# Six shared PSUM banks, attention three chunks ahead and an earlier first layer, in attention followed by a squared-ReLU layer pair

## The chip, the cores and the metric

The kernel runs on one core of a Trainium2 chip. The metric is the time of one execution on the device in microseconds (us). Each kernel was executed several times beside executions of the kernel before on the same chip. The engines are named as in the profile: PE is the matmul engine, DVE the vector engine, ACT the scalar engine, POOL the one that issues the loads, SP the one that issues the stores. PSUM is the memory that the matmuls write to; the kernels here divide it into eight banks, and a pool of PSUM tiles with `bufs=n` holds n tiles in turn. A tile is reused once its last reader is done with it. "Span" is the time from the first to the last instruction of a profiled execution; it was about 2 us less than the time of that execution.

## The reference

Attention over 4 batches of 8 heads, 768 positions, head size 64, with a mask that keeps the first 8 positions and the last 96, and a bias that falls with distance; then two layers on the 3072 tokens of 512 features:

```python
keep = is_global | is_local                      # 8 global keys, 96 local ones
a = softmax(where(keep, q @ k.T / 8 - slope[h] * dist, -1e9))
x = (a @ v).transpose(0, 2, 1, 3).reshape(3072, 512)
h = np.maximum(x @ w_in, 0.0)                    # 512 -> 2048
out = h * h @ w_out                              # 2048 -> 512
```

The kernel computes it in 12 chunks of 256 positions, three to a batch (u = 0, 1, 2). The first chunk of a batch (u = 0) needs no keys or values of other chunks; the other two need a second key tile (`kb`) and a second value tile (`veven`).

## The kernel before

Per chunk, a job list of attention is woven into a job list of the two layers. The schedule is fixed by hand, so the order of jobs is the order of their matmuls on PE: in the timeline below `trk` waits 0.68 us, and the `hps` put down after it starts only then. `later` holds vector work that is put down just before the next job.

```python
ps_sc  = tile_pool("ps_sc",  bufs=2)   # scores: 2 tiles of two banks
ps_ffn = tile_pool("ps_ffn", bufs=3)   # both layers (and the turns of chunks 0 and 1)
ps_att = tile_pool("ps_att", bufs=1)   # ALL other attention tiles: one bank

def turn_q(c): trq = ps_att.tile(...)  # 8 transposes -> ACT copy to qx; later: 2 DVE copies
def turn_k(c): trk = ps_att.tile(...)  # 8 transposes -> ACT copy to kx; later: 4 DVE copies (kb)
def fix_v(c):  ...                     # DVE: vodd and, for u != 0, veven
def score(c, a):
    sp = ps_sc.tile([P, 2, 2, 2, P])   # 8 matmuls
    nc.scalar.activation(out=ex, in_=sp, func=AF.Exp)       # 128x1024
    later.append(phat = ex * mask)                          # DVE
def attend(c, a):
    av = ps_att.tile(...)              # 8 matmuls of phat with V
    rec = 1 / av[..., D]; tm = av * rec                     # DVE
def to_x(c, g):
    trx = ps_att.tile(...)             # 4 matmuls of tm with a permutation -> ACT copy to xt
def first(c, i):                       # 8 matmuls -> ACT relu (hr), later: DVE square (h2)
    ps = ps_ffn.tile(...)
def second(c, j, m0):                  # 4 matmuls of 512 columns; after 16, DVE copy y and store
    if m0 == 0: ck.yps = ps_ffn.tile(...)
# ... cut ...
run(<attention of chunk 0, then of chunk 1>)                # the ramp
run(merge(zip_jobs(f1(0), f1(1)) + f2(0) + f2(1), prep(2) + [fix_v(2)] + att[2], 20, 30))
run(merge(f1(2), prep(3) + [fix_v(3)] + att[3] + prep(4) + [fix_v(4)], 0, 7))
for c in range(2, NC):
    main = zip_jobs(f2(c), f1(c + 1)) if c + 1 < NC else f2(c)
    side = att[c + 2] ...              # with prep(c + 3) and fix_v(c + 3) in between
    run(merge(main, side, 1, len(main) - 2))                # side spread evenly over main
```

The softmax here doesn't subtract the row's maximum and nothing guards it: scores larger than these inputs give would overflow.

Of the kernel before, what the change touches and what calls it, by code (L numbers as in the profile page):

```python
# [8 lines left out]
FP32 = mybir.dt.float32  # L9
# [5 lines left out]
P = 128  # L15
# [3 lines left out]
def merge(main, side, start, stop):  # L19

    out = []
    done = 0
    for i, f in enumerate(main):
        if i >= start:
            want = len(side) if i >= stop else (i - start) * len(side) // (stop - start)
            while done < want:
                out.append(side[done])
                done += 1
        out.append(f)
    return out + side[done:]  # L30
# [3 lines left out]
def kernel(  # L34
# [32 lines left out]
    stage_p = ctx.enter_context(tc.tile_pool(name="stage", bufs=4))  # L67
    sv_p = ctx.enter_context(tc.tile_pool(name="svp", bufs=7))
# [6 lines left out]
    ps_sc = ctx.enter_context(tc.tile_pool(name="ps_sc", bufs=2, space=bass.MemoryType.PSUM))  # L75
    ps_ffn = ctx.enter_context(tc.tile_pool(name="ps_ffn", bufs=3, space=bass.MemoryType.PSUM))
    ps_att = ctx.enter_context(tc.tile_pool(name="ps_att", bufs=1, space=bass.MemoryType.PSUM))
# [9 lines left out]
    dist = const.tile([P, 2, 3, P], FP32, name="dist")  # L87
    loc = const.tile([P, 2, 3, P], FP32, name="loc")
# [15 lines left out]
    def fill_index():  # L104
        nc.gpsimd.iota(pidx, pattern=[[0, 1]], base=0, channel_multiplier=1,
                       allow_small_or_imprecise_dtypes=True)
        for kind, base in ((0, 0), (1, P)):
            for ek in range(2):
                nc.gpsimd.iota(dist[:, ek, kind, :].rearrange("p (e c) -> p e c", e=2),
                               pattern=[[1, 2], [2, HP]], base=base - ek,  # L110
                               channel_multiplier=-2, allow_small_or_imprecise_dtypes=True)
        nc.gpsimd.iota(jmp, pattern=[[1, P]], base=0, channel_multiplier=-2,
                       allow_small_or_imprecise_dtypes=True)

    def fill_masks():
# [14 lines left out]
        V.tensor_scalar(out=dist[:, :, 2, :], in0=dist[:, :, 0, :], scalar1=shift,  # L130
                        scalar2=None, op0=ALU.add)
        for k0, k1, f in ((0, 2, 0), (2, 3, 1)):
            d, l, g = dist[:, :, k0:k1, :], loc[:, :, k0:k1, :], ge0[:, :, k0:k1, :]
            V.tensor_scalar(out=g, in0=d, scalar1=0.0, scalar2=None, op0=ALU.is_ge)
            V.scalar_tensor_tensor(out=l, in0=d, scalar=float(NL), in1=g,
                                   op0=ALU.is_lt, op1=ALU.mult)
            V.scalar_tensor_tensor(out=d, in0=d, scalar=fill[:, f:f + 1], in1=l,
                                   op0=ALU.subtract, op1=ALU.mult)
            V.tensor_scalar(out=d, in0=d, scalar1=fill[:, f:f + 1], scalar2=None,
                            op0=ALU.add)  # L140
        V.tensor_scalar(out=perm, in0=jmp, scalar1=thr, scalar2=None, op0=ALU.is_equal)

# [26 lines left out]
    def load(c, h0=0, h1=H):  # L169
        ck = chunks[c]  # L170
        if h0 == 0:
            ck.sq = stage_p.tile([P, H, P], FP16, name="sq", tag="sq")
            ck.sk = stage_p.tile([P, H, P], FP16, name="sk", tag="sk")
            ck.sv = sv_p.tile([P, H, P], FP16, name="sv", tag="sv")
        for src, dst in ((q, ck.sq), (k, ck.sk), (v, ck.sv)):
            nc.gpsimd.dma_start(  # L176
                out=dst[:, h0:h1, :],
                in_=src[ck.b, h0:h1, ck.u * CH:(ck.u + 1) * CH, :].rearrange(
                    "h (p e) d -> p h (e d)", e=2))

    def turn_q(c, h0=0, h1=H, ramp=False):
        ck = chunks[c]
        if h0 == 0:
# [3 lines left out]
        trp = (ps_ffn.tile([P, H, P], FP16, name="trq", tag="ffn") if ramp  # L187
               else ps_att.tile([P, H, P], FP16, name="trq", tag="att"))
# [261 lines left out]
```

## Time and profile before

| | before |
|---|---|
| three runs | 296.85, 297.13, 301.64 us |
| span of the profiled run, mean granted clock | 300.0 us, 0.965 |
| first matmul of the first layer | 39.6 us |
| a chunk of the steady part, u = 0 / u = 1, 2 | 20.2 / 23.8 us |
| PE work in such a chunk, without waits (summed in the prediction) | 17.8 us |

A run is called slow when it is over 1.5% above the fastest of its kernel; the profiled one (302.07 us) was.

The page of the profiled run. The first line is busy time, share of the span and number of instructions of each engine; the rows below are tenths of busy time, and of the granted matmul clock, in 40 equal slices of the span.

```profile
PE 237.9 (79%) x2208; PEld 157.7 (53%) x2208; DVE 154.5 (51%) x407; ACT 144.4 (48%) x211; POOL 41.0 (14%) x58
...
PE   1353489968757896998897896998897996999995
...
PEclk9999999999997999899998899899999899799999
```

PE is busy for 79%, but its row shows a thin ramp in the first five slices, and the clock row dips to 7 and 8 now and then. The windows view says how much time each stretch has. Its columns are the stretch and its length, then busy time (with the number of instructions) of PE, of PE's weight loads, of DVE, ACT and POOL, then the granted clock, the DMA share and GB/s.

```profile
core 0: us, PE busy (x) PEld busy (x) DVE busy (x) ACT busy (x) POOL busy (x), PEclk, DMA share, GB/s
0.00:39.63 39.63, 15.12 (x177) 11.73 (x178) 21.52 (x64) 21.05 (x34) 22.11 (x37) 1.00 1.25 166
125.40:145.64 20.24, 18.30 (x186) 12.18 (x185) 10.72 (x26) 11.23 (x17) 2.62 (x3) 1.00 0.49 66
145.64:169.47 23.83, 20.00 (x186) 12.85 (x185) 12.91 (x35) 11.34 (x17) 2.62 (x3) 0.93 0.41 56
```

In the first 39.6 us PE works 15. Then a chunk with u = 0 takes 20.2 us and one with u = 1 or 2 takes 23.8, the latter at a clock of 0.93. The timeline of PE inside the last of these shows why (start, length, instructions; in brackets the idle time just ahead of the group and what ended it):

```profile
155.02 0.41 PE L285 MATMUL av<-vodd,phat 128*128 128x65 f16 x8
155.27 1.02 PE L346 MATMUL yps<-w_out_sb,h_1527 128*128 128x512 f16 x4
156.97 0.61 PE L206 MATMUL trk<-ident,sk 128*128 128x128 f16 x8 [0.68 <-DVE tm L292]
157.41 1.04 PE L334 MATMUL hps<-xt,w_in_sb 128*128 128x256 f16 x8
...
162.44 0.40 PE L304 MATMUL trx<-perm,tm 128*128 128x128 f16 x4 [2.00 <-DVE tm L292]
162.68 1.49 PE L346 MATMUL yps<-w_out_sb,h_1527 128*128 128x512 f16 x4
163.95 1.92 PE L334 MATMUL hps<-xt,w_in_sb 128*128 128x256 f16 x8
165.66 1.46 PE L346 MATMUL yps<-w_out_sb,h_1814 128*128 128x512 f16 x4
```

The transposes of k (`trk`) wait 0.68 us for `tm` of an attend that was done a block earlier: they have no use for `tm`, but they share its bank. Then PE idles 2.0 us before the last `trx`, which does need `tm`. And the blocks after it run slow: 1.49 us in place of 1.02 to 1.04, then 1.92, then 1.46. Waits of this kind in the whole run (total us, times, longest):

```profile
PE trx L304 <- DVE tm L292: 13.6, 8, 2.2
...
PE av L285 <- DVE tm L292: 8.9, 13, 1.4
...
PE trk L206 <- DVE tm L292: 4.7, 7, 0.7
```

### The profile page before, as it was taken

What the parts mean: (1) busy time and instruction counts of PE and PEld (TensorE: products, weight loads), DVE (VectorE), ACT (ScalarE), POOL (GpSimd) and SP (SyncE); (2) the same over time, 40 slices, a digit from 0 to 9 for tenths busy, and PEclk for the clock granted to TensorE, in tenths of its full rate; (3) what the DMA queues carried; (4) which work ended last, traced back from release to release, by engine and by line L of the source; (5) the groups of instructions that cost most, each with busy time, mean ns of one, the idle gap of its engine ahead of it and who ended that gap; (6) DMA issues with size and microseconds to landing.
All of it is one profiled execution on the core that took longest, in us unless ns stands there. A gap on an engine that the chain in (4) does not pass through costs nothing.

```text
span 300.0 us, 5337 instructions
## 1 busy us (share of the span) xinstructions
PE 237.9 (79%) x2208; PEld 157.7 (53%) x2208; DVE 154.5 (51%) x407; ACT 144.4 (48%) x211; POOL 41.0 (14%) x58
## 2 busy tenths in 40 slices
PE   1353489968757896998897896998897996999995
PEld 0243368634545564565564464566565564666662
DVE  4565525365363865374466366274466366274321
ACT  0867436353564563464463463464463463363320
POOL 8833350030301212012012000000000000000000
PEclk9999999999997999899998899899999899799999
DMA  7999999193380947019147010000010000000001
GB/s 70 145 206 207 198 181 179 10 120 86 69 79 2 106 50 93 35 8 126 45 70 72 35 38 2 35 0 37 36 37 0 37 35 2 35 37 35 37 35 70
DMA packets 45191, 20.26 MB, mean 68 GB/s; under 512 B 38000, under 2 KB 42096, under 8 KB 45168
## 3 DMA queue, kind: packets, MB, share of 16 engines
q0 software_dynamic: 41712, 13.63, 41.1%
q1 hardware_dynamic: 3456, 6.29, 5.5%
q8 instruction: 17, 0.28, 0.4%
q14 instruction: 6, 0.05, 0.0%
HBM read 27.26 MB, written 6.29 MB: 112 GB/s over the span
## 4 chain that ended last, share of the span: by engine, by line
PE 55%; DVE 21%; ACT 16%; issue 6%; POOL 1%; ACTq 0%; POOLq 0%
PE hps L334 22%; PE yps L346 20%; ACT ex L268 7%; DVE tm L292 5%; DVE phat L271 4%; PE av L285 3%; PE sp L262 3%; ACT hr L337 3%; ACT kx L208 2%; PE trx L304 2%; PE trk L206 2%; PE trq L190 2%; ACT qx L192 1%; DVE rec L290 1%; ACT mask L145 1%
## 5 line engine op out<-in xcount | busy, mean ns | idle before, releaser
L334 PE MATMUL hps<-xt,w_in_sb 128*128 128x256 f16 x768 | 104.4, 286 | 0.0
L337 ACT ACTIVATE hr<-hps 128x512 f16<-128x512 f32 x96 | 57.8, 602 | 85.1 <-PE hps L334 85.1
L334 PEld LDWEIGHTS <-w_in_sb 128*128 128x128 f16 x768 | 75.9, 102 | 18.9 <-issue 2.9
L268 ACT ACTIVATE ex<-sp 128x1024 f16<-128x1024 f32 x48 | 46.5, 1022 | 13.1 <-PE sp L262 13.1
L271 DVE TENSOR_TENSOR phat<-ex,mask 128x1024 f16<-128x1024 f16 x48 | 33.1, 692 | 26.1 <-ACT ex L268 26.0
L285 PE MATMUL av<-vodd,phat 128*128 128x65 f16 x256 | 19.7, 205 | 26.2 <-DVE phat L271 10.5
L285 PEld LDWEIGHTS <-phat 128*128 128x128 f16 x384 | 17.7, 103 | 38.4 <-DVE phat L271 16.5
L350 DVE COPY y<-yps 128x512 f32<-128x512 f32 x24 | 16.5, 689 | 17.5 <-PE yps L346 17.3
L176 POOL DMA_DIRECT2D sq<-in_q_dram x13 | 11.3, 870 | 89.3 <-PE trq L190 83.3
L306 ACT CAST xt<-trx 128x512 f16<-128x512 f32 x24 | 14.1, 587 | 18.2 <-PE trx L304 17.6
L304 PE MATMUL trx<-perm,tm 128*128 128x128 f16 x96 | 10.5, 239 | 13.9 <-DVE tm L292 13.6
L292 DVE TENSOR_TENSOR tm<-av,rec 128x256 f16<-128x256 f32 x48 | 20.4, 424 | 1.7
L262 PE MATMUL sp<-qx,kx 64*128 64x128 f16 x256 | 15.8, 234 | 6.4 <-ACT kx L208 5.8
L208 ACT COPY kx<-trk 128x1024 f16<-128x1024 f16 (+1 forms) x13 | 12.3, 949 | 14.2 <-PE trk L206 14.2
L262 PEld LDWEIGHTS <-kx 64*128 64x128 f16 x256 | 10.5, 102 | 13.7 <-issue 6.7
L304 PEld LDWEIGHTS <-tm 128*128 128x128 f16 x96 | 6.9, 105 | 18.9 <-DVE tm L292 16.6
L192 ACT COPY qx<-trq 128x1024 f16<-128x1024 f16 (+1 forms) x13 | 12.4, 955 | 6.9 <-PE trq L190 6.9
L176 POOL DMA_DIRECT2D sk<-in_k_dram x13 | 11.2, 860 | 21.7 <-PE trk L206 16.1
L290 DVE RECIPROCAL rec<-av 128x4 f32<-128x4 f32 x48 | 8.6, 180 | 9.9 <-PE av L285 9.7
L206 PE MATMUL trk<-ident,sk 128*128 128x128 f16 x96 | 8.4, 234 | 6.5 <-DVE tm L292 4.7
L190 PE MATMUL trq<-ident,sq 128*128 128x128 f16 x96 | 8.4, 234 | 5.5 <-DMA sq<-in_q_dram 4.7
L206 PEld LDWEIGHTS <-sk 128*128 128x128 f16 x96 | 6.5, 105 | 10.8 <-issue 10.2
(82 smaller groups left out, 288.0 us busy)
## 6 DMA issues: line engine op xcount, KB each, us to landing
out_dram<-y SPq DMA_DIRECT2D x24, 256.0 KB, 2.0
sq<-in_q_dram POOLq DMA_DIRECT2D x11, 256.0 KB, 4.7
sk<-in_k_dram POOLq DMA_DIRECT2D x11, 256.0 KB, 6.3
sv<-in_v_dram POOLq DMA_DIRECT2D x11, 256.0 KB, 6.9
w_in_sb<-in_moe_w_in_dram POOLq DMA_DIRECT2D x4, 512.0 KB, 12.7
w_out_sb<-in_moe_w_out_dram POOLq DMA_DIRECT2D x4, 512.0 KB, 18.4
sq<-in_q_dram POOLq DMA_DIRECT2D x2, 128.0 KB, 3.4
sk<-in_k_dram POOLq DMA_DIRECT2D x2, 128.0 KB, 3.5
```

The lines of the kernel that those rows point to most:

```text
L176: nc.gpsimd.dma_start(out=dst[:, h0:h1, :], in_=src[ck.b, h0:h1, ck.u * CH:(ck.u + 1) * CH, :].rearrange("h (p e) d -> p h (e d)", e=2))
L206: nc.tensor.transpose(out=trp[:, h, :], in_=ck.sk[:, h, :], identity=ident)
L208: nc.scalar.copy(out=ck.k[:, hh, :], in_=trp[:, hh, :])
L262: nc.tensor.matmul(sp[:, ek, e, s, :], lhsT=ck.keys[rr][rows, h, :], rhs=ck.q[rows, 1 - ek:3 - ek, h, rr * HP:(rr + 1) * HP], start=True, ...
L268: nc.scalar.activation(out=ex.rearrange("p k e c -> p (k e c)"), in_=sp.rearrange("p k e s c -> p (k e s c)"), func=AF.Exp, scale=scale)
L271: later.append(lambda: nc.vector.tensor_tensor(out=phat, in0=ex, in1=mask[:, :, 2 * a:2 * a + 2, k0:k0 + 2, :].rearrange("p k e s c -> p k ...
L285: nc.tensor.matmul(av[:, e, rr, :], lhsT=phat[:, ek, e, s * P:(s + 1) * P], rhs=ck.vals[rr][:, 2 * a + e, ek, 0:D + 1], start=ek == 0, sto ...
L292: nc.vector.tensor_tensor(out=tm.rearrange("p r e d -> p e r d"), in0=av[:, :, :, 0:D], in1=rec[:, :, :, None].to_broadcast([P, 2, 2, D]), ...
L304: nc.tensor.matmul(trx[:, i, rr, :], lhsT=ck.tm[2 * g + i][:, rr, :, :], rhs=perm, start=True, stop=True)
L334: nc.tensor.matmul(ps[:, m2, :], lhsT=w_in_sb[:, kk, m * P:(m + 1) * P], rhs=ck.xt[:, kk, :], start=kk == 0, stop=kk == NCT - 1)
L337: nc.scalar.activation(out=hr, in_=ps, func=AF.Relu)
L346: nc.tensor.matmul(ck.yps, lhsT=ck.h2[:, m, j * P:(j + 1) * P], rhs=w_out_sb[:, m, :], start=m == 0, stop=m == NFT - 1)
```

## The change

The intent: let attention tiles and first-layer tiles rotate through six single banks, so that none queues behind one bank; put the attention jobs at fixed places between the layer jobs and run them three chunks ahead; and begin the first layer after the attention of chunk 0 alone, with a quarter of w_in loaded ahead of chunk 1. The core of the diff:

```diff
-    ps_sc = ... bufs=2 (two banks each)    ps_ffn = ... bufs=3    ps_att = ... bufs=1
+    ps = ctx.enter_context(tc.tile_pool(name="ps", bufs=6, space=bass.MemoryType.PSUM))
+    ps_y = ctx.enter_context(tc.tile_pool(name="ps_y", bufs=2, space=bass.MemoryType.PSUM))
+    def bank(shape, name, dtype=FP32):
+        return ps.tile(shape, dtype, name=name, tag="bank")
 # trq, trk, av, trx and hps each take bank(...); yps takes ps_y
-        sp = ps_sc.tile([P, 2, 2, 2, P], FP32, name="sp", tag="sc")
+        sp = [bank([P, 2, 2, P], "sp") for _ in range(2)]
-        nc.scalar.activation(out=ex..., in_=sp..., func=AF.Exp, scale=scale)
+        for ek in range(2):
+            nc.scalar.activation(out=ex[:, ek]..., in_=sp[ek]..., func=AF.Exp, scale=scale)
 # ... cut: stage_p 4 -> 3 buffers, sv_p 7 -> 6, ex 3, xt 4; masks of the odd kind made first;
 # ... the first q and k copied by DVE in place of ACT ...
+    ORDER = (0, 2, 3, 1, 6, 4, 5, 7)   # scores 0-3, attend 0, 1, scores 4-7, to_x 0, attend 2, 3, to_x 1
-        load(1);  for c in range(4): load_w_in(...)
+        load_w_in(0, 512);  load(1);  <the other three quarters>
-        run(<attention of chunks 0 and 1>) ... f1(0), f1(1), f2(0), f2(1) with att[2] ...
+        run(<attention of chunk 0>)
+        run(place(f1(0), [lambda: fix_v(1)] + [att[1][i] for i in ORDER] + prep(2),
+                  [1, 0, 2, 3, 4, 5, 6, 6, 7, 6, 7]))
+        run(place(f1(1), [lambda: fix_v(2)] + [att[2][i] for i in ORDER] + prep(3), <same places>))
+        run(place(f2(0), [lambda: fix_v(3)] + [att[3][i] for i in ORDER] + prep(4), <same places>))
+        for c in range(1, NC):
+            main = zip_jobs(f2(c), f1(c + 1)) if c + 1 < NC else f2(c)
+            side = [lambda c=c: fix_v(c + 3)] + [att[c + 3][i] for i in ORDER]
+            slots = [2, 0, 4, 5, 7, 8, 11, 12, 15]     # prep(c + 4) at 2 and 9
+            run(place(main, side, slots))
```

More of the change, by code (lines that the diff above doesn't have):

```diff
@@ L16, with place @@
 HP = P // 2
-def merge(main, side, start, stop):
+def place(main, side, slots):
     out = []
-    done = 0
     for i, f in enumerate(main):
-        if i >= start:
-            want = len(side) if i >= stop else (i - start) * len(side) // (stop - start)
-            while done < want:
-                out.append(side[done])
-                done += 1
+        out += [g for g, s in zip(side, slots) if s == i]
         out.append(f)
-    return out + side[done:]
+    return out
 @with_exitstack
@@ L66 @@
     const = ctx.enter_context(tc.tile_pool(name="const", bufs=1))
-    stage_p = ctx.enter_context(tc.tile_pool(name="stage", bufs=4))
-    sv_p = ctx.enter_context(tc.tile_pool(name="svp", bufs=7))
+    stage_p = ctx.enter_context(tc.tile_pool(name="stage", bufs=3))
+    sv_p = ctx.enter_context(tc.tile_pool(name="svp", bufs=6))
     qk_p = ctx.enter_context(tc.tile_pool(name="qkp", bufs=3))
@@ L74 @@
     y_p = ctx.enter_context(tc.tile_pool(name="yp", bufs=4))
-    ps_sc = ctx.enter_context(tc.tile_pool(name="ps_sc", bufs=2, space=bass.MemoryType.PSUM))
-    ps_ffn = ctx.enter_context(tc.tile_pool(name="ps_ffn", bufs=3, space=bass.MemoryType.PSUM))
-    ps_att = ctx.enter_context(tc.tile_pool(name="ps_att", bufs=1, space=bass.MemoryType.PSUM))
+    ps = ctx.enter_context(tc.tile_pool(name="ps", bufs=6, space=bass.MemoryType.PSUM))
+    ps_y = ctx.enter_context(tc.tile_pool(name="ps_y", bufs=2, space=bass.MemoryType.PSUM))
+    def bank(shape, name, dtype=FP32):
+        return ps.tile(shape, dtype, name=name, tag="bank")
     w_in_sb = const.tile([P, NCT, d_ff], FP16, name="w_in_sb")
@@ L87 @@
     dist = const.tile([P, 2, 3, P], FP32, name="dist")
+    dist0 = const.tile([P, 2, P], FP32, name="dist0")
     loc = const.tile([P, 2, 3, P], FP32, name="loc")
@@ L111, in fill_index @@
                                channel_multiplier=-2, allow_small_or_imprecise_dtypes=True)
+        for ek in range(2):
+            nc.gpsimd.iota(dist0[:, ek, :].rearrange("p (e c) -> p e c", e=2),
+                           pattern=[[1, 2], [2, HP]], base=-ek, channel_multiplier=-2,
+                           allow_small_or_imprecise_dtypes=True)
         nc.gpsimd.iota(jmp, pattern=[[1, P]], base=0, channel_multiplier=-2,
@@ L129, in fill_masks, with fill_even, fill_dist @@
         V.tensor_scalar(out=fill, in0=fill, scalar1=float(NL), scalar2=None, op0=ALU.add)
-        V.tensor_scalar(out=dist[:, :, 2, :], in0=dist[:, :, 0, :], scalar1=shift,
-                        scalar2=None, op0=ALU.add)
-        for k0, k1, f in ((0, 2, 0), (2, 3, 1)):
-            d, l, g = dist[:, :, k0:k1, :], loc[:, :, k0:k1, :], ge0[:, :, k0:k1, :]
-            V.tensor_scalar(out=g, in0=d, scalar1=0.0, scalar2=None, op0=ALU.is_ge)
-            V.scalar_tensor_tensor(out=l, in0=d, scalar=float(NL), in1=g,
-                                   op0=ALU.is_lt, op1=ALU.mult)
-            V.scalar_tensor_tensor(out=d, in0=d, scalar=fill[:, f:f + 1], in1=l,
-                                   op0=ALU.subtract, op1=ALU.mult)
-            V.tensor_scalar(out=d, in0=d, scalar1=fill[:, f:f + 1], scalar2=None,
-                            op0=ALU.add)
-        V.tensor_scalar(out=perm, in0=jmp, scalar1=thr, scalar2=None, op0=ALU.is_equal)
+        V.tensor_scalar(out=perm, in0=jmp, scalar1=thr, scalar2=None, op0=ALU.is_equal)
+    def fill_even():
+        nc.vector.tensor_scalar(out=dist[:, :, 2, :], in0=dist0, scalar1=shift,
+                                scalar2=None, op0=ALU.add)
+        fill_dist(2, 3, 1)
+    def fill_dist(k0, k1, f):
+        V = nc.vector
+        d, l, g = dist[:, :, k0:k1, :], loc[:, :, k0:k1, :], ge0[:, :, k0:k1, :]
+        V.tensor_scalar(out=g, in0=d, scalar1=0.0, scalar2=None, op0=ALU.is_ge)
+        V.scalar_tensor_tensor(out=l, in0=d, scalar=float(NL), in1=g,
+                               op0=ALU.is_lt, op1=ALU.mult)
+        V.scalar_tensor_tensor(out=d, in0=d, scalar=fill[:, f:f + 1], in1=l,
+                               op0=ALU.subtract, op1=ALU.mult)
+        V.tensor_scalar(out=d, in0=d, scalar1=fill[:, f:f + 1], scalar2=None, op0=ALU.add)
     def fill_decay(k0, k1, h0, h1):
@@ L167, with load, turn_q @@
         chunks.append(ck)
-    def load(c, h0=0, h1=H):
+    def load(c, *which):
         ck = chunks[c]
-        if h0 == 0:
-            ck.sq = stage_p.tile([P, H, P], FP16, name="sq", tag="sq")
-            ck.sk = stage_p.tile([P, H, P], FP16, name="sk", tag="sk")
-            ck.sv = sv_p.tile([P, H, P], FP16, name="sv", tag="sv")
-        for src, dst in ((q, ck.sq), (k, ck.sk), (v, ck.sv)):
+        for src in which or (q, k, v):
+            if src is q:
+                dst = ck.sq = stage_p.tile([P, H, P], FP16, name="sq", tag="sq")
+            elif src is k:
+                dst = ck.sk = stage_p.tile([P, H, P], FP16, name="sk", tag="sk")
+            else:
+                dst = ck.sv = sv_p.tile([P, H, P], FP16, name="sv", tag="sv")
             nc.gpsimd.dma_start(
-                out=dst[:, h0:h1, :],
-                in_=src[ck.b, h0:h1, ck.u * CH:(ck.u + 1) * CH, :].rearrange(
+                out=dst, in_=src[ck.b, :, ck.u * CH:(ck.u + 1) * CH, :].rearrange(
                     "h (p e) d -> p h (e d)", e=2))
-    def turn_q(c, h0=0, h1=H, ramp=False):
+    def turn_q(c, h0=0, h1=H, by=None):
         ck = chunks[c]
@@ L186, in turn_q @@
             ck.q = qk_p.tile([P, 3, H, P], FP16, name="qx", tag="qx")
-        trp = (ps_ffn.tile([P, H, P], FP16, name="trq", tag="ffn") if ramp
-               else ps_att.tile([P, H, P], FP16, name="trq", tag="att"))
+        trp = bank([P, H, P], "trq", FP16)
         for h in range(h0, h1):
@@ L191, in turn_q @@
         hh = slice(h0, h1)
-        nc.scalar.copy(out=ck.q[:, 1, hh, :], in_=trp[:, hh, :])
+        (by or nc.scalar.copy)(out=ck.q[:, 1, hh, :], in_=trp[:, hh, :])
         def beside():
@@ L197, in turn_q, with turn_k @@
         later.append(beside)
-    def turn_k(c, h0=0, h1=H, ramp=False):
+    def turn_k(c, h0=0, h1=H, by=None):
         ck = chunks[c]
@@ L202, in turn_k @@
             ck.k = kx_p.tile([P, H, P], FP16, name="kx", tag="kx")
-        trp = (ps_ffn.tile([P, H, P], FP16, name="trk", tag="ffn") if ramp
-               else ps_att.tile([P, H, P], FP16, name="trk", tag="att"))
+        trp = bank([P, H, P], "trk", FP16)
         for h in range(h0, h1):
@@ L207, in turn_k @@
         hh = slice(h0, h1)
-        nc.scalar.copy(out=ck.k[:, hh, :], in_=trp[:, hh, :])
+        (by or nc.scalar.copy)(out=ck.k[:, hh, :], in_=trp[:, hh, :])
         if ck.u == 0:
@@ L262, in score @@
                     nc.tensor.matmul(
-                        sp[:, ek, e, s, :], lhsT=ck.keys[rr][rows, h, :],
+                        sp[ek][:, e, s, :], lhsT=ck.keys[rr][rows, h, :],
                         rhs=ck.q[rows, 1 - ek:3 - ek, h, rr * HP:(rr + 1) * HP],
                         start=True, stop=True)
-        ex = phat_p.tile([P, 2, 2, 2 * P], FP16, name="ex", tag="ex")
+        ex = phat_p.tile([P, 2, 2, 2 * P], FP16, name="ex", tag="ex", bufs=3)
         phat = phat_p.tile([P, 2, 2, 2 * P], FP16, name="phat", tag="phat")
-        nc.scalar.activation(out=ex.rearrange("p k e c -> p (k e c)"),
-                             in_=sp.rearrange("p k e s c -> p (k e s c)"),
-                             func=AF.Exp, scale=scale)
+        for ek in range(2):
+            nc.scalar.activation(out=ex[:, ek].rearrange("p e c -> p (e c)"),
+                                 in_=sp[ek].rearrange("p e s c -> p (e s c)"),
+                                 func=AF.Exp, scale=scale)
         later.append(lambda: nc.vector.tensor_tensor(
@@ L280, in attend @@
         phat = ck.phat[a]
-        av = ps_att.tile([P, 2, 2, D + 1], FP32, name="av", tag="att")
+        av = bank([P, 2, 2, D + 1], "av")
         for e in range(2):
@@ L299, in to_x @@
         if g == 0:
-            ck.xt = h_p.tile([P, NCT, CH], FP16, name="xt", tag="xt")
-        trx = ps_att.tile([P, 2, 2, P], FP32, name="trx", tag="att")
+            ck.xt = h_p.tile([P, NCT, CH], FP16, name="xt", tag="xt", bufs=4)
+        trx = bank([P, 2, 2, P], "trx")
         for i in range(2):
@@ L311, in attention, with both @@
         ck.phat, ck.tm = {}, {}
-        jobs = []
-        for g in range(2):
-            def both(g=g):
-                score(c, 2 * g)
-                score(c, 2 * g + 1)
-            jobs.append(both)
-            if g == 1:
-                jobs.append(lambda: to_x(c, 0))
-            jobs.append(lambda g=g: attend(c, 2 * g))
-            jobs.append(lambda g=g: attend(c, 2 * g + 1))
-        jobs.append(lambda: to_x(c, 1))
-        return jobs
+        def both(g):
+            score(c, 2 * g)
+            score(c, 2 * g + 1)
+        return ([lambda: both(0), lambda: both(1)] + [lambda a=a: attend(c, a) for a in range(4)]
+                + [lambda: to_x(c, 0), lambda: to_x(c, 1)])
     def first(c, i):
@@ L329, in first @@
             ck.h2 = h_p.tile([P, NFT, CH], FP16, name="h2", tag="h2")
-        ps = ps_ffn.tile([P, 2, CH], FP32, name="hps", tag="ffn")
+        hps = bank([P, 2, CH], "hps")
         for m2 in range(2):
@@ L333, in first @@
             for kk in range(NCT):
-                nc.tensor.matmul(ps[:, m2, :], lhsT=w_in_sb[:, kk, m * P:(m + 1) * P],
+                nc.tensor.matmul(hps[:, m2, :], lhsT=w_in_sb[:, kk, m * P:(m + 1) * P],
                                  rhs=ck.xt[:, kk, :], start=kk == 0, stop=kk == NCT - 1)
         hr = h_p.tile([P, 2, CH], FP16, name="hr", tag="hr")
-        nc.scalar.activation(out=hr, in_=ps, func=AF.Relu)
+        nc.scalar.activation(out=hr, in_=hps, func=AF.Relu)
         later.append(lambda: nc.vector.tensor_tensor(
@@ L343, in second @@
         if m0 == 0:
-            ck.yps = ps_ffn.tile([P, d_model], FP32, name="yps", tag="ffn")
+            ck.yps = ps_y.tile([P, d_model], FP32, name="yps", tag="y")
         for m in range(m0, m0 + 4):
@@ L372, in load_w_out, with prep @@
             in_=moe_w_out[m0 * P:m1 * P, :].rearrange("(m p) d -> p m d", p=P))
-    def prep(c, ramp=False):
-        return [lambda: turn_q(c, ramp=ramp), lambda: turn_k(c, ramp=ramp)]
+    def prep(c):
+        return [lambda: turn_q(c), lambda: turn_k(c)]
     engines = {PE, mybir.EngineType.Pool, mybir.EngineType.Activation, mybir.EngineType.DVE}
@@ L379 @@
         fill_ident()
-        load(0, 0, 4)
+        load(0, q)
         fill_index()
-        load(0, 4, 8)
+        load(0, k)
+        load(0, v)
+        load_w_in(0, 512)
         load(1)
-        for c in range(4):
-            load_w_in(c * 512, (c + 1) * 512)
-        for c in range(4):
-            load_w_out(c * 4, (c + 1) * 4)
+        for f in range(512, d_ff, 512):
+            load_w_in(f, f + 512)
         load(2)
+        for m in range(0, NFT, 4):
+            load_w_out(m, m + 4)
@@ L389 @@
         load(3)
         fill_masks()
-        fill_decay(0, 2, 0, 2)
+        fill_dist(0, 2, 0)
+        fill_decay(0, 2, 0, 4)
         att = [attention(c) for c in range(NC)]
-        run([lambda: turn_q(0, 0, 4, True), lambda: turn_k(0, 0, 4, True),
-             lambda: fill_decay(0, 2, 2, 4), att[0][0], lambda: fix_v(0, 0, 4),
-             lambda: turn_q(0, 4, 8, True), lambda: turn_k(0, 4, 8, True),
-             lambda: fill_decay(0, 2, 4, 8), att[0][1], att[0][2], att[0][3],
-             lambda: fix_v(0, 4, 8)] + att[0][4:6] + prep(1, True) + att[0][6:]
-            + [lambda: fill_decay(2, 3, 0, 8), lambda: fix_v(1)] + att[1])
+        dve = nc.vector.tensor_copy
@@ new lines @@
+        run([lambda: turn_q(0, 0, 4, dve), lambda: turn_q(0, 4, 8, dve),
+             lambda: turn_k(0, 0, 4, dve), lambda: turn_k(0, 4, 8, dve),
+             att[0][0], lambda: fill_decay(0, 2, 4, 8), lambda: fix_v(0), att[0][2], att[0][1],
+             lambda: fill_even(), att[0][3], att[0][6], lambda: turn_q(1), att[0][4],
+             lambda: turn_k(1), att[0][5], att[0][7], lambda: fill_decay(2, 3, 0, 8)])
+        run(place(f1(0), [lambda: fix_v(1)] + [att[1][i] for i in ORDER] + prep(2),
+                  [1, 0, 2, 3, 4, 5, 6, 6, 7, 6, 7]))
@@ L399 @@
         load(4)
-        run(merge(zip_jobs(f1(0), f1(1)) + f2(0) + f2(1),
-                  prep(2) + [lambda: fix_v(2)] + att[2], 20, 30))
+        run(place(f1(1), [lambda: fix_v(2)] + [att[2][i] for i in ORDER] + prep(3),
+                  [1, 0, 2, 3, 4, 5, 6, 6, 7, 6, 7]))
         load(5)
-        run(merge(f1(2), prep(3) + [lambda: fix_v(3)] + att[3] + prep(4) + [lambda: fix_v(4)],
-                  0, 7))
-        load(6)
-        for c in range(2, NC):
+        run(place(f2(0), [lambda: fix_v(3)] + [att[3][i] for i in ORDER] + prep(4),
+                  [1, 0, 2, 3, 4, 5, 6, 6, 7, 6, 7]))
@@ L409 @@
             main = zip_jobs(f2(c), f1(c + 1)) if c + 1 < NC else f2(c)
-            side = att[c + 2] if c + 2 < NC else []
+            side, slots = [], []
             if c + 3 < NC:
-                p = prep(c + 3) + [lambda c=c: fix_v(c + 3)]
-                side = side[:4] + p[:1] + side[4:6] + p[1:] + side[6:]
-            run(merge(main, side, 1, len(main) - 2))
+                side = [lambda c=c: fix_v(c + 3)] + [att[c + 3][i] for i in ORDER]
+                slots = [2, 0, 4, 5, 7, 8, 11, 12, 15]
+            if c + 4 < NC:
+                side += prep(c + 4)
+                slots += [2, 9]
+            run(place(main, side, slots))
 _INS = ['q', 'k', 'v', 'n_global', 'n_local', 'moe_w_in', 'moe_w_out']
```

## The prediction

> What bounds the kernel now. The chain of waits gives PE 55%, DVE 21%, ACT 16%, but stretches differ. In the windows view the first 40 us (attention of chunks 0 and 1) have PE busy 15.5 us; the first layer starts at 39.6 us in the timeline. Then a chunk takes 20.2 us where it opens a batch and 23.8 us in the other two of three. Its PE work, start to start in the timeline, is less: eight first-layer matmuls 0.87 us, four second-layer ones 0.86, sixteen scores 0.62, eight of attention times V 0.28, four to x 0.28, eight transposes 0.45: 16 x 0.868 + 3.9 = 17.8 us. The rest waits on the single attention bank (av and trx groups wait for DVE tm: 14.3, 8.9, 13.6 us in the waits), with a 2.0 us idle before trx in every 23.8 us chunk. After it the next blocks run slow (second-layer 1.49 us for 1.03, first-layer 1.92 for 1.04; granted clock 0.93 in those windows, 1.00 in the 20.2 us ones): 1.7 us more. The Trainium skill ("TensorE: Matmul & The Clock Gate", HAM oscillation) names idle gaps of over about 3.4 us as what re-throttles; here 2.0 us was followed by it.
>
> What the change does. The single attention bank goes: attention tiles and the first layer share six. The exponential (1.02 us) is split in two of about 0.60: ACT gains 48 x 0.18 = 9 us busy, off the path (ACT is 48% busy). Copies of the first q and k move to DVE; a quarter of w_in is loaded before chunk 1; chunk 1's attention moves out of the ramp into the first layer of chunk 0. Matmuls, bytes and vector work hardly change.
>
> Sum, by walking the new instruction order with the old durations:
> - Ramp: masks ready at about 6.4 us (was 8.2), then the DVE/ACT chain of chunk 0. First layer starts at about 27 us, 12 earlier.
> - Three stages with eight main blocks each (10.9 us of PE work, but 12 on ACT, 12.5 on DVE, and a chain exp, phat, fix_v, tm, then the banks of the next scores): about 19, 16.5 and 14.5 us; ends near 77 us. PE waits about 17 us here.
> - Eight chunks at 18.4 us (0.6 of waits, mostly av banks held while DVE does fix_v): 147.
> - Chunks 9 and 10 at 13.9, the last second layer 6.95, tail 3.65 (as before): 38.5.
> Span about 262.5, plus 2.1 (profiled run 302.07, span 300.0): 264. DMA should not bind: w_in landed by 20 to 28 us before, w_out by 38, needed at about 62.
>
> Nearly all of it is critical, as PE is the floor: 27 + 209.7 + 3.65 + 2.1 = 242 would be perfect.
>
> Prediction 263 us, 254 to 273. Faster by over 2%: 0.97; within 2%: 0.02; slower: 0.01.
>
> Signs that would show it right: first hps at 26 to 30 us; in chunks 1 to 8 a period of 18 to 18.8 us, with ACT hr waiting for PE and PE hardly for anything; no clock dip and no 2 us idle before trx; ex 0.60 us x 96; the longest PE idle between 27 and 77 us, waiting on DVE tm or phat.
>
> What would make it wrong: banks taken in order stall PE behind DVE's fix_v in every chunk (period 19.5 or more: +9 us); the low-duty stages until 77 us run at a low clock (+3 to 6); loads of w_in or chunk 1 come late; or the three first stages overlap better than my walk (-8).

## The result, and the profile after

| | before | after |
|---|---|---|
| runs | 296.85, 297.13, 301.64, 302.4 us | 265.19, 265.24, 267.16, 267.31 us |
| median | 299.38 us | 266.2 us |
| span, mean clock of the profiled run | 300.0 us, 0.965 | 265.4 us, 0.974 |

The ratio is 0.8964 (95% interval 0.8882 to 0.9046). All ratios here are the mean time of one kernel's fast runs over that of the other's fast runs of the same rounds (one group of experiments departs from that, as said there), so they are not quite the ratio of the medians quoted. The result is faster by 10%, and 266.2 us lies inside the predicted range of 254 to 273.

The same lines of the page:

```profile
PE 224.8 (85%) x2208; PEld 155.6 (59%) x2208; DVE 156.4 (59%) x410; ACT 143.8 (54%) x255; POOL 39.7 (15%) x57
...
PE   1335579498878998999998989999989979999994
...
PEclk9999759979999999999999999999999999999999
```

PE's busy share rose to 85% while its busy time fell by 13 us for the same 2208 matmuls; matmuls at a low clock count as longer busy time. The clock row has dips left at slices 5, 6 and 9 only. It doesn't show all of the slow matmuls, though: in the ramp it reads full, and yet the sixteen scores at 10.36 us took 1.03 us, where sixteen at 64.73 us took 0.62. So a low clock is read below from durations as well. The profile of before is one of a slow execution and this one of a fast one, so the sizes of single stretches are compared with that in mind. The windows of the changed kernel, columns as before; the stages are cut at the first score matmul of each:

```profile
0.00:26.32 26.32, 8.93 (x105) 7.18 (x106) 16.80 (x48) 12.25 (x20) 16.55 (x31) 1.00 1.25 153
26.32:47.88 21.56, 15.55 (x154) 11.51 (x153) 11.79 (x33) 14.14 (x29) 7.42 (x9) 0.76 1.55 193
47.88:64.73 16.85, 13.15 (x152) 10.20 (x153) 10.54 (x28) 10.78 (x20) 1.72 (x2) 0.90 0.53 53
64.73:78.61 13.88, 10.98 (x120) 6.20 (x121) 8.72 (x23) 7.55 (x13) 3.55 (x5) 1.00 0.66 79
78.61:97.65 19.04, 17.89 (x185) 12.44 (x186) 13.10 (x35) 10.99 (x19) 2.63 (x3) 1.00 0.87 105
116.71:134.27 17.56, 17.56 (x187) 12.46 (x186) 11.63 (x30) 11.37 (x20) 2.63 (x3) 1.00 0.56 76
```

The lines are, in order: the ramp; the first layer of chunk 0 with attention 1; the first layer of chunk 1 with attention 2; the second layer of chunk 0 with attention 3; then a chunk with u != 0 and one with u = 0 of the steady part. The walk in the prediction had 27, 19, 16.5, 14.5 us and 18.4 on average for the last two. The first stage came out 2.6 us longer. Its timeline shows waits for V, with slow matmuls before and after them:

```profile
26.87 3.35 PE L335 MATMUL hps<-xt,w_in_sb 128*128 128x256 f16 x16
33.37 0.24 PE L291 MATMUL av<-vodd,phat 128*128 128x65 f16 x2 [3.15 <-DVE vodd L248]
34.85 0.27 PE L291 MATMUL av<-veven,phat 128*128 128x65 f16 x2 [1.24 <-DVE veven L251]
...
35.15 1.90 PE L335 MATMUL hps<-xt,w_in_sb 128*128 128x256 f16 x8
...
37.29 1.90 PE L335 MATMUL hps<-xt,w_in_sb 128*128 128x256 f16 x8
```

Eight first-layer matmuls take 1.90 us here where they otherwise take 1.04, and the first sixteen take 3.35 where sixteen at 48.44 us take 1.92. The wait of 3.15 us isn't due to the place of `fix_v` alone: DVE makes `vodd` after two `phat`, and waits 4.4 us for their exponentials, which stand on ACT behind eight exponentials of the masks (2.56 us, from 26.90 us). In the steady part the one wait left is again for V:

```profile
82.22 1.04 PE L335 MATMUL hps<-xt,w_in_sb 128*128 128x256 f16 x8
83.43 0.24 PE L291 MATMUL av<-vodd,phat 128*128 128x65 f16 x2 [0.17 <-DVE vodd L248]
84.65 0.22 PE L291 MATMUL av<-veven,phat 128*128 128x65 f16 x2 [0.99 <-DVE veven L251]
```

A chunk with u = 0 has no PE wait at all: PE is busy 17.56 us of 17.56. The waits in the whole run that answer to those of before:

```profile
PE av L291 <- DVE veven L251: 8.2, 8, 1.2
...
PE trx L310 <- DVE tm L298: 6.6, 5, 4.2
...
PE av L291 <- DVE vodd L248: 6.1, 6, 3.1
```

The wait of transposes for `tm` is gone from the list, and so is that of `av` for `tm`. What is left for `trx` is the ramp and small pieces. New are 8.2 us for `veven` and 6.1 for `vodd`: DVE builds these in `fix_v`, which the new order puts between the first scores and the first attend.

### The profile page after: what moved, and what is told of

It is laid out like the page before. It is cut to its first block, busy times and chain, and to the rows that moved or that the text cites. A ratio compares the mean times of both kernels' runs of the same rounds, so it can differ in the third digit from the quotient of the medians.

```text
span 265.4 us, 5380 instructions
## 1 busy us (share of the span) xinstructions
PE 224.8 (85%) x2208; PEld 155.6 (59%) x2208; DVE 156.4 (59%) x410; ACT 143.8 (54%) x255; POOL 39.7 (15%) x57
## 4 chain that ended last, share of the span: by engine, by line
PE 62%; DVE 17%; ACT 16%; issue 3%; POOL 1%; POOLq 0%; ACTq 0%
PE yps L347 26%; PE hps L335 25%; ACT ex L274 9%; PE av L291 5%; DVE phat L277 3%; PE sp L267 3%; ACT hr L338 2%; PE trx L310 2%; DVE vodd L244 2%; ACT mask L151 2%; DVE veven L251 1%; DVE veven L250 1%; DVE vodd L248 1%; PE trk L211 1%; ACT kx L213 1%
## 5 line engine op out<-in xcount | busy, mean ns | idle before, releaser
L338 ACT ACTIVATE hr<-hps 128x512 f16<-128x512 f32 x96 | 58.6, 614 | 80.2 <-PE hps L335 80.0
L335 PEld LDWEIGHTS <-w_in_sb 128*128 128x128 f16 x768 | 73.8, 100 | 19.4 <-issue 0.3
L274 ACT ACTIVATE ex<-sp 128x512 f16<-128x512 f32 x96 | 49.5, 605 | 11.7 <-PE sp L267 11.7
L291 PEld LDWEIGHTS <-phat 128*128 128x128 f16 x384 | 19.0, 102 | 28.0 <-issue 9.1
L291 PE MATMUL av<-veven,phat 128*128 128x65 f16 x128 | 11.5, 197 | 8.2 <-DVE veven L251 8.2
L198 ACT COPY qx<-trq 128x1024 f16<-128x1024 f16 x11 | 11.4, 1038 | 1.9 <-PE trq L196 1.9
L213 ACT COPY kx<-trk 128x1024 f16<-128x1024 f16 x11 | 11.7, 1060 | 0.3 <-PE trk L211 0.3
L184 POOL DMA_DIRECT2D sv<-in_v_dram x12 | 10.7, 893 | 2.8 <-DMA w_out_sb<-in_moe_w_out_dram 1.3
L196 PEld LDWEIGHTS <-sq 128*128 128x128 f16 x96 | 6.8, 106 | 5.8 <-DMA sq<-in_q_dram 5.6
## 6 DMA issues: line engine op xcount, KB each, us to landing
w_out_sb<-in_moe_w_out_dram POOLq DMA_DIRECT2D x4, 512.0 KB, 17.8
```

Source lines behind the costliest of these rows:

```text
L184: nc.gpsimd.dma_start(out=dst, in_=src[ck.b, :, ck.u * CH:(ck.u + 1) * CH, :].rearrange("h (p e) d -> p h (e d)", e=2))
L196: nc.tensor.transpose(out=trp[:, h, :], in_=ck.sq[:, h, :], identity=ident)
L274: nc.scalar.activation(out=ex[:, ek].rearrange("p e c -> p (e c)"), in_=sp[ek].rearrange("p e s c -> p (e s c)"), func=AF.Exp, scale=scale)
L291: nc.tensor.matmul(av[:, e, rr, :], lhsT=phat[:, ek, e, s * P:(s + 1) * P], rhs=ck.vals[rr][:, 2 * a + e, ek, 0:D + 1], start=ek == 0, sto ...
L335: nc.tensor.matmul(hps[:, m2, :], lhsT=w_in_sb[:, kk, m * P:(m + 1) * P], rhs=ck.xt[:, kk, :], start=kk == 0, stop=kk == NCT - 1)
L338: nc.scalar.activation(out=hr, in_=hps, func=AF.Relu)
```

## The experiments

Nine kernels were run: eight changed ones, each profiled and timed in three rounds (four executions), all of them correct, and the kernel before once more for a second profile. They ran in three groups, not all on the same chip; each ratio is to executions of the kernel before on the same chip, which lay at 297 to 302.5 us. In the group of experiments 3, 6, 7 and 8 three of the seven executions of the kernel before are marked slow, and the recorded ratios, given as such, nevertheless answer to a mean of 300.9 us that includes them. Against the four fast ones alone (mean 299.1 us) they are 0.942, 0.890, 0.815 and 0.806, and these are used where experiments are compared.

### 1. The new order with the old banks

```diff
 # in the changed kernel
-    ps (6 banks), ps_y (2 banks)
+    ps_sc (4 single banks: sp), ps_ffn (3: hps, yps, turns of chunks 0 and 1), ps_att (1: all else)
```

> The changed kernel's order with the banks of before: four for scores, three for both layers, one for all other attention tiles (the turns of chunks 0 and 1 use the layers' banks, as before). Theory (order and banks each give a part: the order the earlier start and the spacing that removes the 2 us idle before trx, the banks the waits between attention tiles): 270 to 279 us, first layer still starts at 26 to 28 us, the waits PE <- DVE tm come back at av, trx and transposes, with 0.3 to 1 us more in each of chunks 1 to 8. Rival A (the order alone does it, the banks matter little): 264 to 268 us. Rival B (the single bank was the limit): 283 us or more.

Measured: 293.42 us median (292.53 to 294.86), ratio to before 0.9836 (0.9758 to 0.9915). The expected 270 to 279 us was missed by far, and rival B (283 us or more) fits. The first layer did start at 27.7 us, 12 us earlier than before, and still almost nothing was gained. A steady chunk with u = 1 took 20.9 us, against 19.0 with six banks. The timeline of PE in it:

```profile
118.06 1.02 PE L349 MATMUL yps<-w_out_sb,h 128*128 128x512 f16 x4
119.77 0.24 PE L293 MATMUL av<-vodd,phat 128*128 128x65 f16 x2 [0.69 <-DVE tm L300]
...
123.53 1.03 PE L349 MATMUL yps<-w_out_sb,h 128*128 128x512 f16 x4
125.38 0.61 PE L213 MATMUL trk<-ident,sk 128*128 128x128 f16 x8 [0.83 <-ACT xt L314]
```

The second attend of a pair waits 0.69 us for the bank of the first, and the transposes of k wait 0.83 us for the copy that empties the bank of `trx`. The first three stages took 25.5, 20.5 and 18.1 us, against 21.6, 16.9 and 13.9: these are stages with twice as many attention jobs per layer job, so the single bank costs most per stage there (11.8 us of the 25.4 by which the two spans differ). About half of the 11.8 is slow matmuls: PE is busy 45.4 us in the three stages against 39.7, for the same number of matmuls, at clocks of 0.77, 0.83 and 0.86 against 0.76, 0.90 and 1.00. So the theory that the order gives a large part by itself fell.

### 2. The new banks with the old order

```diff
 # in the kernel before
-    ps_sc (2 x two banks), ps_ffn (3), ps_att (1)
+    ps (6 single banks: sp in two, trq, trk, av, trx, hps), ps_y (2: yps)
 # and the exponential in two halves; order, ramp and loads as before
```

> Before's order, ramp and loads with the six banks in rotation and the split exponential. Theory: the first layer starts at 37 to 40 us as before; the 2 us idle before trx stays, as it waits for the data of the last tm and not for a bank; 283 to 293 us. Rival A (order alone): 295 to 300 us, nothing gained. Rival B (banks): 275 us or less, no idle before trx.

Measured: 275.02 us median (272.3 to 275.47), ratio 0.9196 (0.9113 to 0.9279). This too missed the expected 283 to 293 us, on the other side: rival B's time (275 or less) is what came out. But rival B's sign was not there: the idle before the last `trx` stayed, 1.90 us.

```profile
147.94 0.28 PE L305 MATMUL trx<-perm,tm 128*128 128x128 f16 x2
150.11 0.28 PE L305 MATMUL trx<-perm,tm 128*128 128x128 f16 x2 [1.90 <-DVE tm L293]
150.24 1.03 PE L347 MATMUL yps<-w_out_sb,h 128*128 128x512 f16 x4
151.10 1.04 PE L335 MATMUL hps<-xt,w_in_sb 128*128 128x256 f16 x8
```

The first two of the four `trx` matmuls go as soon as their `tm` is there, and the last two wait for theirs. So that idle is a wait for data, as the theory had it. What the banks took away in this order are the waits of transposes and attends for `tm` and most of the low clock in the steady chunks: of the five idles there of 1.9 to 2.1 us before `trx`, only one was followed by slow blocks. A chunk with u != 0 without such a dip took 20.5 us in place of 23.8, with a clock of 1.00; about 1.7 us of the difference is the low clock, as a chunk of the kernel before without a dip took 22.1 us (experiment 9). In the ramp and the first layer the clock still dipped (0.87 and 0.92), so the mean of the run, 0.969, tells nothing of this.

With both runs, the four corners are: neither 1, order alone 0.984, banks alone 0.920, both 0.896. The banks (with the exponential in halves in the old order) are worth 8 to 9% in either order, the order (with its ramp and loads) 1.6% on the old banks, where the interval reaches from 0.8 to 2.4%, and about 3% on the new. The last comes from the times, 275.0 and 266.2 us, which were not taken side by side; the quotient of the ratios gives 2.5%, but the fast runs of before averaged 297.0 us for the changed kernel and 298.4 us for these two.

### 3. Two attention banks in the kernel before

```diff
-    ps_ffn = ... bufs=3    ps_att = ... bufs=1
+    ps_ffn = ... bufs=2    ps_att = ... bufs=2
```

> The kernel before with two banks for the attention tiles and two in place of three for the layers; nothing else. Theory (what the banks gain is that transposes, av and trx no longer queue one behind the other on one bank): most of the 24 us that six banks gained in that order, 275 to 286 us, PE waits for DVE tm at av gone, the 2 us before the last trx still there. Rival (a deep rotation shared with the first layer is needed, two banks only move the wait to hps): 290 us or more.

Measured: 281.9 us median (281.13 to 282.17), recorded ratio 0.9363 (0.9311 to 0.9415), 0.942 against the fast runs, inside the expected range. Moving one bank from the layers to attention, a change of two figures, gives a gain of 5.8%, where six banks give 8.0% in this order. The wait for `tm` at `av` is gone, that before `trx` stays, and the price of the bank is a new wait of 1.00 us in each of seven chunks: the next second-layer tile waits for the copy `y`.

```profile
151.48 0.29 PE L304 MATMUL trx<-perm,tm 128*128 128x128 f16 x2 [1.89 <-DVE tm L292]
151.61 1.03 PE L346 MATMUL yps<-w_out_sb,h 128*128 128x512 f16 x4
...
164.60 1.02 PE L346 MATMUL yps<-w_out_sb,h 128*128 128x512 f16 x4 [1.00 <-DVE y L350]
```

The five idles of 1.9 to 2.1 us before `trx` are there, and not one is followed by slow blocks (mean clock of the run 1.00). The waits in the steady chunks are only a small part of the gain: a chunk with u != 0 took 21.7 us, against 22.1 without a dip in the kernel before, so the eight chunks give about 4 of the 19 to 20 us by which the spans differ from the two profiles of before. The rest is dips that did not come (5 to 8.5 us there) and the time ahead of the steady part, where attention 4 begins at 92.8 us in place of 100.7 and 103.0.

### 4. V tiles one stage earlier

```diff
 # in the changed kernel
-                side = [lambda c=c: fix_v(c + 3)] + [att[c + 3][i] for i in ORDER]
-                slots = [2, 0, 4, 5, 7, 8, 11, 12, 15]
+                side = [att[c + 3][i] for i in ORDER]
+                slots = [0, 4, 5, 7, 8, 11, 12, 15]
-                side += prep(c + 4);  slots += [2, 9]
+                side += prep(c + 4) + [lambda c=c: fix_v(c + 4)];  slots += [2, 9, 14]
 # likewise fix_v(1) at the end of the ramp, fix_v(2), (3), (4) at place 7 of the first three stages
```

> The changed kernel with the V tiles of each chunk built one stage earlier, after the last scores, in place of between the first scores and the first attend. Theory (the 1.2 to 1.5 us by which chunks with u not 0 take longer than the 17.5 us of the others is PE waiting for veven and vodd, and in the first three stages this wait and the low clock after it cost more): no PE wait for veven or vodd, all chunks 1 to 8 at 17.4 to 17.8 us, 252 to 260 us. Rival (DVE is so full that the work only moves the wait to tm, phat or the squares): 263 us or more.

Measured: 248.22 us median (247.58 to 249.06), ratio 0.8319 (0.8254 to 0.8385), better than the theory's range by 4 us. The three stages after the ramp and the first steady chunk (a u != 0 one):

```profile
26.36:43.94 17.58, 13.08 (x155) 10.34 (x154) 11.53 (x33) 14.10 (x29) 7.39 (x9) 0.90 1.49 196
43.94:56.83 12.89, 11.47 (x153) 9.21 (x154) 10.68 (x29) 10.74 (x20) 1.73 (x2) 1.00 1.27 126
56.83:69.38 12.55, 10.83 (x121) 6.21 (x122) 8.30 (x23) 7.55 (x13) 3.78 (x5) 1.00 0.71 84
69.38:86.92 17.54, 17.54 (x184) 12.44 (x186) 12.98 (x37) 11.00 (x19) 2.63 (x3) 1.00 0.94 114
```

Each of the steady chunks takes 17.55 us and PE has no recorded wait in any of them. DVE is busy 12 to 13 us of 17.5, so there was room; only the place of the work was wrong. The rival (DVE too full) is refuted. Against the changed kernel, 9.3 us of the gain of 18 is in the first three stages, which shrank from 21.6, 16.9 and 13.9 to 17.6, 12.9 and 12.6 us, and nearly all the rest is the 1.3 to 1.5 us in each of six steady chunks.

### 5. Attention two chunks ahead

```diff
 # in the changed kernel
-        run(place(f1(1), ... att[2] ...));  run(place(f2(0), ... att[3] ...))
-        for c in range(1, NC):   ... att[c + 3], fix_v(c + 3), prep(c + 4)
+        for c in range(0, NC):   ... att[c + 2], fix_v(c + 2), prep(c + 3)
```

> The changed kernel with attention two chunks ahead: the stages of f1(1) with attention 2 and f2(0) with attention 3 (16.9 + 13.9 us) are replaced by one ordinary period of f2(0) with f1(1) and attention 2, and one more later period of 13.9 us without attention gains an attention. Theory (three ahead buys no slack that the periods use; its two half-filled stages cost): 10 periods of 18.6 on average and one of 13.9 in place of 30.7 + 8 x 18.6 + 2 x 13.9, so 7 us less: 257 to 262 us. Rival (three ahead is needed as slack; at two ahead PE stalls at the boundary on xt or kx): 265 us or more.

Measured: 258.96 us median (258.73 to 259.24), ratio 0.8679 (0.8603 to 0.8756): 7 us less than the changed kernel, as expected. Its first full period, the second layer of chunk 0 with the first of chunk 1 and attention 2, took 19.05 us and replaced the two stages of 16.85 and 13.88; later chunks took as long as in the changed kernel. Running three ahead bought nothing: it only added two stages in which eight layer blocks cannot cover the chain of a whole attention.

### 6. The load order of before

```diff
-        load_w_in(0, 512);  load(1);  <three quarters of w_in>
+        load(1);  <four quarters of w_in>
```

> The changed kernel with the first quarter of w_in loaded after chunk 1, as before. Theory (the first layer waits for the attention of chunk 0, not for w_in, which landed by 20 us with the load order of before and is first used at 26.9 us): same as the changed kernel, 264 to 268 us; first hps at 26 to 27.5 us. Rival (the early quarter is what lets the first layer begin so soon): first hps at 28 us or later and 268 us or more.

Measured: 266.54 us median (264.64 to 266.93), recorded ratio 0.8836 (0.8771 to 0.8901), 0.890 against the fast runs: the same time as the changed kernel, whose 0.896 is to faster runs of before (297.0 us). The first layer began at 26.91 us, against 26.87. The early quarter of w_in does nothing here; the start waits for the attention of chunk 0.

### 7. Both edits of 4 and 5

The edits are those two, with `fix_v(c + 3)` at place 14 of each period.

> Both edits: V tiles a stage early and attention two chunks ahead. Theory (the two gains are of different waits): V early alone has the stages f1(1) and f2(0) at 12.9 + 12.6 us and periods of 17.55 without any PE wait; replacing them by one period of 17.55 and lengthening one of 13.9 by 3.65 saves 4.2 us: 242 to 246 us. Rival (two ahead leaves V, prepared late in the period before, too little time): 248 us or more.

Measured: 243.96 us median (243.09 to 244.6), recorded ratio 0.8105 (0.8056 to 0.8153), 0.815 against the fast runs. That is 4.3 us less than experiment 4, as expected. It is less than the 7.2 us of experiment 5, as V tiles made early had already shortened the two stages that fall away (12.9 and 12.6 us for 16.9 and 13.9).

### 8. And the masks of the second kind moved

```diff
 # in the kernel of 7, in the ramp
+             lambda: fill_even(),                       # DVE, ahead of the first scores
              att[0][0], lambda: fill_decay(0, 2, 4, 8), lambda: fix_v(0), att[0][2], att[0][1],
-             lambda: fill_even(), att[0][3], att[0][6], ...
+             lambda: fill_decay(2, 3, 0, 8), att[0][3], att[0][6], ...
-             att[0][7], lambda: fill_decay(2, 3, 0, 8)])
+             att[0][7]])
```

> The former, and the decay masks of the second kind moved: their distances made before the first scores of chunk 0 and their eight exponentials (2.6 us of ACT) put behind the second scores of chunk 0, where ACT idled 3.7 us, in place of behind the ramp, where the exponentials of chunk 1 queued behind them. Theory: chunk 0's second tm is no longer behind 2 us of mask work on DVE, the first layer starts 1 to 2 us sooner, and the first attend of chunk 1 follows its scores 2 us sooner: 3 to 4.5 us less, 238 to 241.5 us. Rival (the ramp is bound by the chain scores, exp, phat, av, tm and the copies of chunk 1, and the masks only move): within 1 us of the former.

Measured: 241.05 us median (240.85 to 241.25), recorded ratio 0.801 (0.7967 to 0.8053), 0.806 against the fast runs. The time is in the expected range and the gain of 2.9 us just under the expected 3 to 4.5: the first score of chunk 1 came 1.3 us sooner (24.81 us) and its stage took 15.5 us in place of 17.4. The clock column reads 1.00 there in place of 0.80, but the matmuls were not faster for it: the first sixteen of the first layer took 3.60 us, after 3.10 in experiment 7. PE idled less, 1.8 us for 3.3. The ramp, that stage and the first full period:

```profile
0.00:24.81 24.81, 9.16 (x105) 7.21 (x106) 17.16 (x51) 14.47 (x28) 15.97 (x30) 1.00 1.22 153
24.81:40.35 15.54, 13.77 (x154) 10.83 (x154) 11.40 (x33) 11.93 (x21) 6.25 (x7) 1.00 1.44 198
40.35:57.89 17.54, 17.54 (x184) 12.43 (x185) 12.41 (x31) 10.99 (x19) 4.37 (x5) 1.00 1.70 180
```

This is the fastest version: 19% less than the fast runs of before and 25 us less than the changed kernel.

### 9. A second profile of the kernel before

> The kernel before, unchanged, to have its profile in the fast state if it falls there (the first profile was slow: 300.0 us, clock 0.965). Theory (the slow state of this kernel is the clock dips after the 2 us idle before trx, and fast executions have fewer of them): a span of about 295 us with the same 1.9 to 2.2 us idle before trx and the clock below 1.00 in fewer than five of the six 23.8 us chunks. Rival (the dips are in all of them and the 3 to 5 us lie elsewhere, in the ramp): the same dips in all six.

Measured: 300.74 us in its one run, so it did not fall at the fast end, and the question about the fast state is not answered the way it was meant. But it shows the dips come and go. Here is one of its idles before `trx`:

```profile
163.09 0.40 PE L304 MATMUL trx<-perm,tm 128*128 128x128 f16 x4 [2.00 <-DVE tm L292]
163.32 1.03 PE L346 MATMUL yps<-w_out_sb,h 128*128 128x512 f16 x4
164.18 1.04 PE L334 MATMUL hps<-xt,w_in_sb 128*128 128x256 f16 x8
```

The same 2.00 us idle, and the blocks after it run at full speed; that chunk took 22.1 us, not 23.8. In this profile three of five such idles were followed by slow blocks, in the first profile five of five. Each dip costs about 1.7 us, so their number can move the time by several us from one execution to the next. That this is the whole of the spread from 297 to 302 us was not shown, as no profile fell at 297.

## Why the prediction was right

The time, 266.2 us for 263, and its terms, read from the spans:

| term | predicted | measured |
|---|---|---|
| ramp | 27 | 26.3 |
| three first stages | 19 + 16.5 + 14.5 = 50 | 21.6 + 16.9 + 13.9 = 52.3 |
| eight steady chunks | 147 | 148.3 |
| the rest to the end | 38.5 | 38.5 |
| span | 262.5 | 265.4 |

- The ramp was right: the first layer started at 26.9 us (predicted about 27), and the chain of chunk 0 over PE, DVE and ACT set it (its start does wait for data: the transposes of k for `sk` until 8.48 us), not the loads of w_in. Experiment 6 shows that the early quarter of w_in had no part in it, as the prediction's remark on DMA implied.
- The mis-sized term is the first stage, 21.6 us for 19. The prediction named a low clock in the thin stages only as a risk. It happened: between 34.9 and 40.5 us blocks ran at half speed, which against their usual lengths costs about 2.7 us (two blocks of 0.87 us start to start took 1.68 and 1.83, a third 1.22, sixteen scores 0.97 for 0.56, eight of attention times V 0.46 for 0.28). But a second term was left out: the walk put 12 us on ACT in such a stage, and the trace has 14.1, as the eight exponentials of the masks (2.56 us) run ahead of those of the scores, and PE waits behind them. How much of the 2.6 us each of the two made is not separated; with the masks moved away (experiment 8) the stage was 1.8 us shorter, with its first matmuls as slow as before.
- The steady term was right in size and wrong in mechanism. The prediction had "0.6 of waits, mostly av banks held while DVE does fix_v" in every chunk. The trace shows chunks with u != 0 longer by 1.3 to 1.5 us, 1.0 to 1.2 of it as idle time of PE, and no wait in the others, and PE waits there for `veven` and `vodd` themselves, not for a bank. That the size came out is in part luck: the work was put at 17.8 us a chunk and is 17.56, which offset the waits that were put too low. Experiment 4 settles it: with `fix_v` moved and the banks untouched, all of it goes. The walk had put PE at the first attend without asking whether V was ready.
- The exponential in two halves was put at 9 us more of ACT, off the path. ACT's busy time for it rose by 3.0 us (46.5 to 49.5), since four in a row overlap: 2.06 us for four of 0.605. The Trainium skill ("ScalarE: Activation LUTs", What ACT_TABLE_LOAD costs) says that back-to-back instructions overlap by about 93 ns; this trace gives (4 x 0.605 - 2.06) / 3 = 0.12 us, and the trace of before 2 x 1.022 - 1.94 = 0.10 us for its longer ones.
- Of the signs that the prediction named, the start of the first layer, the exponentials of 0.605 us and the missing idle before `trx` came. Three did not: the clock dips in slices 5, 6 and 9, the chunks take 17.56 or 18.8 to 19.1 us and not 18 to 18.8, and the longest idle of PE between 27 and 77 us (3.15 us) waits for `vodd` and not for `tm` or `phat`.
- "12 us earlier" for the first layer was right and was no gain of 12 us, as the walk already had it: the attention of chunk 1 moved from the ramp into a stage that cannot cover it. Experiment 1 shows the extreme, 12 us earlier and 1.6% gained.
- What the prediction did not attempt is to split the gain over the parts of the change, and my first guess at it, in the expectations of experiments 1 and 2, was wrong. The banks are most of it. "Perfetto Trace Analysis" of the skill (Optimizing Tensor Performance, Matmuls) advises that independent groups rotate through different banks so that the emptying of one overlaps the next; the trace agrees, with 8% for it in experiment 2. The single bank cost more than its own waits in the list: in the one profile each of experiments 2 and 3, most or all of the low clock in the steady chunks went with it. Why it went was not tested by itself.

## What to carry to other kernels

When tiles of different jobs share one PSUM bank, look in the waits for matmuls that wait for a result which they do not use: moving a single bank to them can be worth more than a new order (5.8% here for two figures, against 1.6% for the new order on the old banks). When work is woven into fixed places, check each operand of each job against the time at which it is made, not the banks alone: one vector job placed after the first scores rather than a stage earlier cost 18 of 266 us. And check the clock by the durations of matmuls of one form: its column can read full where they are slow. Starting a bottleneck engine sooner, or running a side job further ahead, gains only what the stages in between can cover.

## What the Trainium skill lacked or had wrong

- "TensorE: Matmul & The Clock Gate" (HAM oscillation) gives the rule to allow no PE idle of over about 3.4 us. Here, in the steady chunks, idles of 2.0 to 2.2 us were followed by blocks at half speed in 8 of 10 cases (two profiles of the kernel before), at about 1.7 us each. With the waits on the single bank taken away, and others of up to 1.0 us still there, idles of 1.9 to 2.1 us were followed by them in 1 of 10 (experiments 2 and 3). So neither the rule nor the length of one idle decides it. The page's second failure mode, frequent short idles (psum-queue depth-cycling), may be the better fit, but it has no figure of how much short idle is too much, and these runs do not settle it.
- "Perfetto Trace Analysis" (Matmul Optimizations) says to use all eight PSUM banks. All kernels here use eight; how they are shared out alone made 5.8% (experiment 3). Beyond the rotation that it advises for matmul groups, the page doesn't name the sign of a wrong share seen here: matmuls that wait for a result which they do not use.
- "ScalarE: Activation LUTs" (What ACT_TABLE_LOAD costs): 186 + 0.833 N ns, for an immediate scale and bias, gives an estimate of 612 ns for 512 elements, and 605 was measured: no fault. The overlap of two in a row was 0.10 to 0.12 us, where the page has about 93 ns.
